# Seven-product expert blocks: sums behind the first layer on VectorE, first half's output sent a block later without drains, token rounding two blocks ahead

## The chip, the cores and the metric

One core of one Trainium2 chip runs one program. The metric is the device time of that program in microseconds; the time before is the median of three runs.

## The reference

```python
q_pool = q.reshape(B, H, S // 2, 2, D).mean(axis=3)          # B, H, S, D = 8, 8, 1152, 64
attn = softmax(q_pool @ k.T / sqrt(D))
x = (attn @ v) as (4608, 512) tokens
logits = x @ w_gate + modality_bias[modality_id]             # 8 experts
e_idx, gate_w = argmax(logits), its softmax probability
out[mask] = gate_w * (relu(x[mask] @ w1[e]) @ w2[e])         # per expert, w1 512x1024, w2 1024x512
```

All inputs and the output are float32.

## The kernel before, in words

The first two thirds of the time are the attention, in which TensorE is busy throughout; the change touches nothing there. Behind it stand the experts (function `experts`, L1375 on). The tokens are routed to experts and sorted into blocks of 256 tokens of one expert. `run_blocks` handles 18 such blocks and one with 32 leftover tokens. Every number is carried as a float16 high half and a float16 low half, so a product of two matrices takes three passes of TensorE (high x high, high x low, low x high).

Blocks 0 to 3 are plain blocks: four groups of first-layer products (`gemm1`) and four of the second layer (`gemm2`), which are the steps s = 0 to 7 of the loop. Blocks 4 to 17 replace the eight half-size products of each layer by seven, with sums of matrix quarters before and behind them (Winograd's form). Blocks 4 to 12 use one set of prepared weights (`sets[0]`), blocks 13 to 17 another (`sets[1]`). A set is prepared by `combined` (L1430): four quarters of a weight are loaded by SyncE into the pool `wr` of five raw buffers, GpSimd makes sums of them (L1433), and each of seven matrices is split: the high half by ScalarE (L1426), the low half by VectorE (L1427).

A block's tokens are prepared by `turn_s` (L1526), a generator of four steps: gates copied and the tokens scaled (ScalarE, `xr`, L1533); four subtractions on GpSimd (L1536); the cast to the high half (ScalarE, `xs`, L1540); the low half (VectorE, L1542) and two transposing DMAs of SyncE into `xpart` (L1545), a tile with two buffers. `load_x` gathers the tokens of a block with two indirect DMAs of GpSimd.

The loop over j from 4 to 17 works on two blocks at once. `together(j, j+1)` issues the first three first-layer products of block j+1 and then the seven second-layer products of block j (`second`); it yields six times, the steps s = 0 to 5. `tail(j+1)` issues the other four first-layer products and yields four times. So TensorE's order is: products 11, s2, s3 of block j+1 into banks `pa`, `pb`, `pc`; second-layer products 11, 22, 12, s3, s1, s2, s4 of block j; products 12, s1, 22, s4 of block j+1. Behind a first-layer product stand `first_sum` (VectorE, L1623), a relu (ScalarE, L1624), and, at the end of `tail`, four sums of the results (L1648, on GpSimd): `hs3`, `h21` (used as s1), `h11` (as s2) and `h12` (as s4). `put_hi` casts a result's high half (ScalarE, L1614), `put_lo` makes its low half (VectorE, L1618); `sums` does both for one of the four.

In `second`, ScalarE takes two scaled copies `p11`, `p12` of the first bank (L1718, `p` in the trace) before the third product adds into it, and another, `x5`, before the seventh product adds into that bank; VectorE adds up the output (L1719), and one quarter is added by GpSimd (L1741). `scatter` (L1592) writes half a block of output rows to the output with an indirect DMA of GpSimd; each scatter waits until the one before it has landed. In the loop the second half of block j is sent at step 4 of `together`, the first half in step 0 of `tail`, followed by `nc.gpsimd.drain`.

The order on TensorE, VectorE, ScalarE and GpSimd is the order of the program (`manual_schedule`); SyncE's DMAs are placed by the scheduler. PREP says how many steps of weight preparation run at each step s: its first part for the plain blocks, its second one tuple for each j from 4 on. T_TURN gives the steps at which block j+3's tokens advance, T_GX the step of the gather for block j+4.

Of the kernel before, what the change touches and what calls it, by code (L numbers as in the profile page):

```python
# [22 lines left out]
P = 128  # L23
# [88 lines left out]
GP = 10  # L112
WR = 5
JOINED = 2
PREP = ((1,) * 8, ((0, 1, 1, 0, 0, 0),) * 6 + ((0,) * 6, (1,) * 6, (1,) * 6) + ((1, 1, 1, 0, 0, 1),) * 4)
T_TURN = (0, 3, 5)
T_GX = 3
SIDE = 1
PH = 3
PO = 2  # L120
GX = 3
T_AHEAD = (6, 7)
T_OWN = ((1, 2), (2, 3))
T_ST = 5
LX = 0
SW = 3
PR = 2
# [42 lines left out]
def drain(g):  # L170
    for _ in g:
        pass
# [1202 lines left out]
def experts(tc, ctx, rt, ident, pre, x2pool, hip, w1, w2, out, side, first):  # L1375
# [54 lines left out]
    def combined(k, w, o, rooms):  # L1430

        rooms = iter(rooms)
        add = lambda o, a, b, op: nc.gpsimd.tensor_tensor(o, a, b, op=op)  # L1433
        put = lambda n, t: o.__setitem__(n, split(t, next(rooms)))
        if w is w1:
            c, a = load(k, w, 2), load(k, w, 3)
            yield
            t = wr.tile([P, 4 * TB], F32, name="raw", tag="w")
            add(t, c, a, ALU.add)
            b = load(k, w, 0)  # L1440
            yield
            put("22", a)
            d = load(k, w, 1)
            yield
            put("s1", t)
            yield
            add(c, b, c, ALU.subtract)
            yield
            put("s3", c)
            yield  # L1450
            add(t, t, b, ALU.subtract)
            yield
            put("11", b)
            yield
            put("s2", t)
            yield
            put("12", d)
            yield
            add(d, d, t, ALU.subtract)
            yield  # L1460
            put("s4", d)
            yield
        else:
            b, a = load(k, w, 1), load(k, w, 0)
            yield
            t = wr.tile([P, 4 * TB], F32, name="raw", tag="w")
            add(t, b, a, ALU.subtract)
            c = load(k, w, 3)
            yield
            put("11", a)  # L1470
            d = load(k, w, 2)
            yield
            put("t1", t)
            yield
            add(b, b, c, ALU.subtract)
            yield
            put("t3", b)
            yield
            add(t, c, t, ALU.subtract)
            yield  # L1480
            put("22", c)
            yield
            put("t2", t)
            yield
            put("21", d)
            yield
            add(d, d, t, ALU.subtract)
            yield
            put("t4", d)
            yield  # L1490
# [94 lines left out]

    def scaled(j, h):
        b = B[j]
        o = b["o", h] = xp.tile([P, DM], F32, name=f"o{h}", bufs=1)
        nc.scalar.activation(o, b["po"][h], AF.Copy, scale=b["gate"][:, h:h + 1])

    def scatter(j, h, n=P):
# [34 lines left out]
    def tail(j):  # L1626

        b = B[j]
        b["H"] = {}
        pa, pb, pc, u2, u3 = (b[n] for n in ("pa", "pb", "pc", "u2", "u3"))  # L1630
        product1(pa, "12", "21", j, False)
        h11 = b["h11"] = temp("h11")
        nc.scalar.activation(h11, pa, AF.Relu)
        yield
        product1(pb, "s1", "t1", j, True)
        first_sum(j, "h22", pb, u3)
        put_hi(j, "11", h11)
        yield
        product1(pc, "22", "t4", j, True)
        first_sum(j, "h12", pc, u3)  # L1640
        put_lo(j, "11", h11)
        put_hi(j, "22", b["h22"])
        yield
        product1(pb, "s4", "22", j, False)
        first_sum(j, "h21", pb, u2)
        h22, h12, h21 = (b[n] for n in ("h22", "h12", "h21"))
        b["hs3"] = temp("hs3")
        sub = lambda o, x, y, op=ALU.subtract: nc.gpsimd.tensor_tensor(o, x, y, op=op)  # L1648
        sub(b["hs3"], h21, h11)
# [8 lines left out]
    def sums(j, n):  # L1658
        t = B[j][dict(s3="hs3", s1="h21", s2="h11", s4="h12")[n]]
        put_hi(j, n, t)  # L1660
        put_lo(j, n, t)

    def together(i, j, scaling=iter(())):

        def mine(n):
            if i is not None:
                sums(i, n)

        if j is not None:
            b = B[j]  # L1670
            pa = b["pa"] = bank()
            product1(pa, "11", "11", j, True)
            p1 = temp("p1")
            nc.scalar.copy(p1, pa)  # L1674
            beside()
            step(scaling)
            mine("s3")
            pb = b["pb"] = bank()
            product1(pb, "s2", "t2", j, True)
# [4 lines left out]
            mine("s1")  # L1684
        else:
            mine("s3")
            mine("s1")
# [21 lines left out]
    def second(j):  # L1709
# [1 line left out]
        b = B[j]  # L1711
        g1, g2 = b["gate"][:, 0:1], b["gate"][:, 1:2]
        half = lambda n: temp(n, TB)
        o1, o2 = (xp.tile([P, DM], F32, name=f"o{h}", bufs=1) for h in range(2))
# [55 lines left out]
    def few_second(j):  # L1770
# [24 lines left out]
        for i in range(2):  # L1795
# [4 lines left out]
        o = b["o", 0] = xp.tile([P, DM], F32, name="o0", bufs=1)  # L1800
# [29 lines left out]
    def run_blocks():  # L1830
# [5 lines left out]
        raws = [load(0, w2, q) for q in range(4)]  # L1836
        load_x(1)
        turn = {1: turn_x(1)}
        prep = chain(combined(1, w1, sets[0]["w1"], (4, 5, 6, 7, 8, 13, 14)), combined(1, w2, sets[0]["w2"], (15, 16, 17, 18, 19, 20, 0)))
        for j in plain:  # L1840
            k = j + 2
            for s in range(8):
# [8 lines left out]
                beside()  # L1851
                if j == 0 and s in (1, 2):
                    step(turn[1])
                if j:
                    step(prep, PREP[0][s])
                if j and s == T_ST:
                    scatter(j - 1, 1)
                    nc.gpsimd.drain(fusable=False)
                if k <= NSA and s == GX:
                    load_x(k)  # L1860
                    turn[k] = (turn_x if k < NSA else turn_s)(k)
                if s in T_AHEAD and k <= NSA:
                    step(turn[k])
                if j == NSA - 1:
                    if s < 3:
# [4 lines left out]
                    if s > 3:  # L1870
                        step(turn[NSA + 1])
                    if s == 6:
                        load_x(NSA + 2)
            if j + 1 < NSA:
                drain(turn[j + 1])
# [12 lines left out]
                turn[k] = turn_s(k)  # L1888
        drain(together(None, j))
        step(turn[j + 2])  # L1890
        load_x(j + 3)
        step(turn[j + 2])
        scatter(j - 1, 1)
        for s, _ in enumerate(tail(j)):
            beside()
            if s == 1:
                step(turn[j + 2])
        drain(turn[j + 2])
        nc.gpsimd.drain(fusable=False)
        prep = chain(combined(0, w1, sets[1]["w1"], (1, 2, 3, 9, 10, 11, 12)), combined(0, w2, sets[1]["w2"], (7, 8, 6, 13, 5, 4, 14)), few_weights())  # L1900
        few_x_ = few_x()
        few1, few2 = few_first(NST), few_second(NST)
        for j in range(NSA, NST):
            if j == last:
                drain(few1)
            x = turn.get(j + 3, iter(()))
            for s, _ in enumerate(together(j, j + 1 if j < last else None, x)):
                beside()
                if s in T_TURN:
                    step(x)  # L1910
                if s == T_GX and j + 4 <= last:
                    if j + 4 == NA:
                        drain(side)
                    load_x(j + 4)
                if j == last - 1:
                    step(few_x_)
                step(prep, PREP[1][j - NSA][s] if j < last else 0)
                if s == 4:
                    scatter(j, 1)
            if j < last:  # L1920
                for s, _ in enumerate(tail(j + 1)):
                    beside()
                    beside()
                    if s == 0:
                        scatter(j, 0)
                        nc.gpsimd.drain(fusable=False)
        scatter(last, 0)
        nc.gpsimd.drain(fusable=False)
        drain(few2)
# [141 lines left out]
```

## Time and profile before

| | us |
|---|---|
| median of three runs | 1171.76 (1169.91 to 1172.52) |
| the profiled execution's own time | 1172.89 |
| its span, first to last instruction | 1171.2 |
| TensorE busy in the span | 1071.8 |
| GpSimd busy in the span | 639.9 |
| mean granted clock of TensorE | 0.97 |

The span is split into engines' busy times; a wait stands before the instruction that waited, with the instruction or DMA that released it. Releasers are inferred, and "issue" means that the profile shows none. The granted clock is the share of TensorE's full speed of 2.4 GHz.

### The profile page before, as it was taken

How to read it: one execution, taken by the hardware profiler on the slowest of the kernel's cores; microseconds unless marked ns; L12 is line 12 of the kernel's file. 1: busy time of each engine (PE TensorE's matmuls, PEld its weight loads, DVE VectorE, ACT ScalarE, POOL GpSimd, SP SyncE). 2: the span in 40 equal slices, each digit the busy share in tenths (PEclk: the TensorE clock that was granted, in tenths of full speed). 3: DMA queues.
4: the chain of work that ended last, by engine and by line, in shares of the span. 5: the costliest groups of instructions: out<-in, count | busy, mean ns of one | idle time of the engine just before them, and what ended most of it. 6: DMA issues, size and time to landing. Idle time of an engine off the chain costs nothing. (4 is left out here: it accounts for less than half of the span.)

```text
span 1171.2 us, 39664 instructions
## 1 busy us (share of the span) xinstructions
PE 1071.8 (92%) x16809; PEld 857.0 (73%) x16809; DVE 967.6 (83%) x1778; ACT 872.9 (75%) x1506; POOL 639.9 (55%) x610
## 2 busy tenths in 40 slices
PE   7999999999999999999999999997687789668985
PEld 3777777777777777777777779887676679567884
DVE  7999999999999999999999976895576666676773
ACT  5899999999999999999999985445545445545542
POOL 7855535445454554454554322477676666767443
PEclk9999999999999999999999999999989889889998
DMA  7688987886988787888788455445544335435210
GB/s 229 177 198 202 200 170 202 194 212 176 203 187 189 195 195 176 209 187 173 195 184 180 125 143 163 139 148 122 120 87 87 72 92 115 129 107 125 69 56 22
DMA packets 181868, 180.19 MB, mean 154 GB/s; under 512 B 113999, under 2 KB 144735, under 8 KB 181680
## 3 DMA queue, kind: packets, MB, share of 16 engines
q1 hardware_dynamic: 171414, 149.22, 52.7%
q0 software_dynamic: 10256, 28.33, 10.7%
q8 instruction: 133, 2.18, 0.8%
q14 instruction: 55, 0.45, 0.1%
q10 hardware_dynamic: 10, 0.00, 0.0%
HBM read 100.30 MB, written 18.98 MB: 102 GB/s over the span
## 5 line engine op out<-in xcount | busy, mean ns | idle before, releaser
L1024 ACT ACTIVATE Pe<-psc 128x432 int32<-128x432 f32 x768 | 376.4, 527 | 41.1 <-PE psc L1023 26.1
L1082 PE MATMUL xp<-VH,Pe 128*128 128x65 f16 x2880 | 345.3, 194 | 1.0 <-issue 1.0
L1083 PE MATMUL xp<-vl,Pe 128*128 128x64 f16 x2880 | 343.9, 192 | 0.5 <-issue 0.5
L1084 PE MATMUL xp<-VS,Pl 128*128 128x65 f16 x2880 | 343.3, 193 | 0.9 <-issue 0.5
L1082 PEld LDWEIGHTS <-Pe 128*128 128x128 f16 x2880 | 266.5, 97 | 94.2 <-issue 51.2
L947 DVE TENSOR_REDUCE mp<-pm 128x2 f32<-128x1024 f32 (+3 forms) x319 | 296.9, 938 | 19.7 <-PE pm L965 15.8
L1022 PE MATMUL psc<-B 128*128 128x432 f16 (+2 forms) x1152 | 302.2, 286 | 1.3 <-ACT Pe L1024 1.2
L1023 PE MATMUL psc<-B 128*128 128x432 f16 (+2 forms) x1152 | 299.6, 285 | 2.3 <-DMA B<-mr 2.3
L1083 PEld LDWEIGHTS <-Pe 128*128 128x128 f16 x2880 | 265.9, 98 | 44.1 <-issue 1.5
L1084 PEld LDWEIGHTS <-Pl 128*128 128x128 f16 x2880 | 266.2, 97 | 0.5 <-DVE Pl L1007 0.5
L1005 ACT ACTIVATE Pl<-Pe 128x1152 f16<-128x1152 uint16 x186 | 216.5, 1164 | 5.9
L868 POOL TENSOR_SCALAR VH<-rawv,sc 128x512 f16<-128x512 f32 (+1 forms) x60 | 104.0, 1733 | 42.4 <-DVE Pl L1007 37.9
L1023 PEld LDWEIGHTS <-B 128*128 128x128 f16 x1152 | 112.5, 98 | 10.5 <-issue 2.7
L1022 PEld LDWEIGHTS <-B 128*128 128x128 f16 x1152 | 111.2, 97 | 7.8 <-issue 2.4
L729 POOL TENSOR_TENSOR rawq<-rawq 128x576 f32<-128x576 f32 x31 | 43.7, 1409 | 118.8 <-DVE Pl L1007 113.3
L776 POOL TENSOR_TENSOR lo<-rawk,hi 128x576 f16<-128x576 f32 (+1 forms) x68 | 81.7, 1221 | 42.4 <-DVE Pl L1007 33.7
L1007 DVE TENSOR_SCALAR Pl<-Pe 128x576 f16<-128x576 uint16 (+1 forms) x198 | 93.1, 472 | 7.2 <-ACT Pe L1024 4.9
L947 DVE TENSOR_REDUCE mp<-xp 128x1 f32<-128x512 f32 x116 | 79.0, 681 | 0.0
L965 PE MATMUL pm<-hi,qh 64*128 64x512 f16 x348 | 70.0, 383 | 1.1 <-DVE mp L947 1.1
L1648 POOL TENSOR_TENSOR h<-h,h 128x512 f32<-128x512 f32 x42 | 64.0, 1524 | 3.3
L1536 POOL TENSOR_TENSOR xr<-xr 128x256 f32<-128x256 f32 x56 | 58.1, 1056 | 6.6 <-DVE w20l L1427 2.6
L1618 DVE TENSOR_TENSOR hs3l<-hs,hs3h 128x512 f16<-128x512 f32 x14 | 16.0, 1144 | 50.8 <-ACT hs3h L1614 50.8
(533 smaller groups left out, 2582.4 us busy)
## 6 DMA issues: line engine op xcount, KB each, us to landing
B<-hi SPq DMA_DIRECT2D x128, 144.0 KB
rawv<-in_att_dram SPq DMA_DIRECT2D x32, 576.0 KB
rawq<-in_att_dram SPq DMA_DIRECT2D x31, 576.0 KB
rawk<-in_att_dram SPq DMA_DIRECT2D x31, 576.0 KB
raw<-in_w_dram SPq DMA_DIRECT2D x28, 512.0 KB
B<-qh SPq DMA_DIRECT2D x128, 72.0 KB
B<-lo SPq DMA_DIRECT2D x64, 144.0 KB
xs<-x SPq DMA_DIRECT2D x15, 576.0 KB
```

The source lines that it names most:

```text
L776: done = (nc.gpsimd if p < 2 or i in LO_POOL else nc.vector).tensor_tensor(o[:, r], t[:, r], h[:, r], op=ALU.subtract)
L868: done = nc.gpsimd.tensor_scalar(vh, v, s["sc"], None, op0=ALU.mult)
L947: most = lambda o, x: nc.vector.tensor_reduce(o, x, op=ALU.max, axis=AX.X)
L965: nc.tensor.matmul(banks[to], queries(j, what), hi[half[j], t * 512:(t + 1) * 512], start=True, stop=True)
L1005: nc.scalar.activation(low, rest, AF.Copy, scale=LOW)
L1007: fast[0] = (nc.vector if eng == 'D' else nc.gpsimd).tensor_single_scalar(low, rest, LOW, op=ALU.mult)
L1022: nc.tensor.matmul(o, b1[:, ks], b1[:, qs], start=True, stop=False, skip_group_check=True)
L1023: nc.tensor.matmul(o, b2[:, ks], b2[:, qs], start=False, stop=True, skip_group_check=True)
L1024: nc.scalar.activation(Pe[:, D + x0:D + x1], pt, AF.Exp, scale=1.0 / 16)
L1082: nc.tensor.matmul(out, Ph[:, qs], vh[:, c, j, 0:D + 1], start=c == 0 and g == 0, stop=False, skip_group_check=True)
L1083: nc.tensor.matmul(out[:, 0:D], Ph[:, qs], vl[:, c, j], start=False, stop=False, skip_group_check=True)
L1084: nc.tensor.matmul(out, Pl[:, qs], vs[:, c, j, 0:D + 1], start=False, stop=c == NKC - 1, skip_group_check=True)
```

## The change

The four sums in `tail` go from GpSimd to VectorE, the fourth into `together`; `put_hi` and `put_lo` are interleaved by hand in `together` in place of `sums`. The first half of block j's output is sent at step 0 of block j+1, from a tile `o0` of two buffers; the drains in the loops are gone, and one is added before the last first half. In block j the tokens of block j+2 take their last two steps at step 0, those of block j+3 their first two at step 3, and the gather for block j+4 moves to step 4. Weight preparation starts in plain block 0, has steps in `tail`, is spread anew over the blocks, and makes two of its GpSimd sums in one step; the rooms that it writes to are numbered anew.

```diff
-PREP = ((1,) * 8, ((0, 1, 1, 0, 0, 0),) * 6 + ((0,) * 6, (1,) * 6, (1,) * 6) + ((1, 1, 1, 0, 0, 1),) * 4)
-T_TURN = (0, 3, 5)
-T_GX = 3
+PREP = (((0, 0, 0, 1, 1, 0, 1, 1), (1, 0, 1, 1, 1, 2, 0, 1), (1, 1, 0, 1, 1, 1, 0, 1), (1, 1, 2, 0, 1, 0, 0, 0)),
+        ((1, 0, 0, 0, 0, 1) + (0,) * 4, (0, 1, 1) + (0,) * 7, (0, 0, 0, 0, 0, 1) + (0,) * 4, (0, 1, 1) + (0,) * 7, (0, 1, 1, 0, 0, 1) + (0,) * 4,
+         (0, 1, 0, 0, 0, 2) + (0,) * 4, (0, 0, 0, 0, 0, 0) + (0,) * 4, (0, 1, 2, 0, 0, 1) + (0,) * 4, (0, 1, 1, 2, 0, 0, 0, 0, 0, 1)) + ((1, 1, 1, 0, 0, 1) + (0,) * 4,) * 4)
+T_NEAR = (0, 0)
+T_FAR = (3, 3)
+T_ST = 2
...
-T_ST = 5
...
     def combined(k, w, o, rooms):
...
+        if one:
+            add(c, b, c)
+            add(t, t, b)
         else:
...
+            add(c, c, b)
+            add(t, b, t)
+        yield
+        put(t3, c)
...
-        o = b["o", h] = xp.tile([P, DM], F32, name=f"o{h}", bufs=1)
+        o = b["o", h] = xp.tile([P, DM], F32, name=f"o{h}", bufs=2 - h)
...
-        sub = lambda o, x, y, op=ALU.subtract: nc.gpsimd.tensor_tensor(o, x, y, op=op)
+        sub = lambda o, x, y, op=ALU.subtract: nc.vector.tensor_tensor(o, x, y, op=op)
+        put_lo(j, "22", h22)
+        put_hi(j, "12", h12)
         sub(b["hs3"], h21, h11)
         sub(h21, h21, h22, ALU.add)
-        put_lo(j, "22", h22)
-        put_hi(j, "12", h12)
         put_lo(j, "12", h12)
         sub(h11, h21, h11)
-        sub(h12, h12, h11)
-        yield
...
     def together(i, j):
...
             nc.scalar.copy(p1, pa)
             beside()
-            step(scaling)
-            mine("s3")
+        hi("s3")
+        lo("s3")
+        hi("s1")
+        if i is not None:
+            nc.vector.tensor_tensor(B[i]["h12"], B[i]["h12"], B[i]["h11"], op=ALU.subtract)
+        lo("s1")
+        hi("s2")
+        if j is not None:
             pb = b["pb"] = bank()
...
         next(g, None)
-        mine("s2")
+        lo("s2")
+        hi("s4")
+        lo("s4")
         next(g, None)
-        mine("s4")
...
-                if j:
-                    step(prep, PREP[0][s])
+                step(prep, PREP[0][j][s])
                 if j and s == T_ST:
                     scatter(j - 1, 1)
-                    nc.gpsimd.drain(fusable=False)
...
-                    if s == 6:
+                    if s == 5:
                         load_x(NSA + 2)
...
-            x = turn.get(j + 3, iter(()))
-            for s, _ in enumerate(together(j, j + 1 if j < last else None, x)):
+            near, far = (turn.get(j + n, iter(())) for n in (2, 3))
+            for s, _ in enumerate(together(j, j + 1 if j < last else None)):
                 beside()
-                if s in T_TURN:
-                    step(x)
...
+                if s == 0 and j > NSA:
+                    scatter(j - 1, 0)
+                if s in T_NEAR and j + 2 <= last:
+                    step(near, T_NEAR.count(s))
+                step(prep, PREP[1][j - NSA][s] if j < last else 0)
+                if s in T_FAR:
+                    step(far, T_FAR.count(s))
+                if s == 4:
+                    scatter(j, 1)
+                    if j + 4 <= last:
...
             if j < last:
                 for s, _ in enumerate(tail(j + 1)):
                     beside()
                     beside()
-                    if s == 0:
-                        scatter(j, 0)
-                        nc.gpsimd.drain(fusable=False)
+                    step(prep, PREP[1][j - NSA][6 + s])
+        nc.gpsimd.drain(fusable=False)
         scatter(last, 0)
         nc.gpsimd.drain(fusable=False)
```

## Rows read from the trace of the kernel before

**Rows 1.** The page: busy time of each engine over the whole span
```profile
PE 1071.8 (92%) x16809; PEld 857.0 (73%) x16809; DVE 967.6 (83%) x1778; ACT 872.9 (75%) x1506; POOL 639.9 (55%) x610
```

**Rows 2.** Stretches: us; PE, PEld, DVE, ACT, POOL busy (count); granted clock; DMA share; GB/s
```profile
750.50:773.90 23.40, 21.76 (x213) 19.29 (x211) 22.98 (x48) 9.51 (x14) 9.49 (x6) 1.00 0.36 114
...
795.30:817.30 22.00, 15.37 (x242) 15.00 (x241) 8.95 (x12) 11.68 (x16) 17.01 (x17) 0.92 0.67 133
...
817.30:1145.60 328.30, 264.28 (x3305) 240.95 (x3303) 222.07 (x283) 163.24 (x266) 217.43 (x165) 0.92 0.40 95
...
973.10:991.80 18.70, 18.64 (x255) 17.57 (x253) 14.76 (x20) 11.05 (x19) 13.64 (x12) 1.00 0.39 92
...
1056.40:1076.50 20.10, 18.69 (x256) 17.62 (x253) 15.87 (x22) 12.56 (x20) 13.96 (x11) 1.00 0.46 125
...
1102.20:1121.40 19.20, 18.76 (x257) 17.64 (x254) 14.73 (x19) 10.45 (x18) 9.03 (x8) 1.00 0.20 52
...
1121.40:1145.60 24.20, 18.98 (x280) 17.02 (x278) 17.20 (x24) 10.92 (x21) 11.19 (x10) 0.93 0.16 46
```

**Rows 3.** Waits, 817.3 to 1145.6 us: total, times, longest
```profile
PE po L1707 <- ACT p L1718: 33.1, 10, 6.9
...
ACT hs3h L1614 <- POOL hs L1648: 32.8, 10, 7.0
...
POOL hs L1648 <- issue: 25.5, 7, 4.9
...
PE ph L1606 <- DVE h L1623: 16.1, 7, 8.4
```

**Rows 4.** Timeline of one block's start on POOL, ACT and PE
```profile
989.41 1.01 POOL L1592 DMA_INDIRECT out_dram<-o,siB  x1 [2.69 <-DVE h L1623]
...
993.92 1.26 POOL L1648 TENSOR_TENSOR hs<-h,h 128x512 f32<-128x512 f32 x1 [3.51 <-issue]
...
995.22 0.62 ACT L1614 CAST hs3h<-hs 128x512 f16<-128x512 f32 x1 [3.40 <-POOL hs L1648]
...
997.08 0.83 ACT L1718 ACTIVATE p<-po,gate 128x256 f32<-128x256 f32 x2
...
997.97 0.27 PE L1707 MATMUL po<-w20h,h12h 128*128 128x256 f16 x1 [3.34 <-ACT p L1718]
```

**Rows 5.** Drains behind the scatters of the first halves, ns min/median/max
```profile
L1926 POOLq DRAIN  x13: 3177/4447/6024, 837.9 to 1139.2; - x13
```

**Rows 6.** VectorE groups, 817.3 to 1145.6 us
```profile
L1542 DVE TENSOR_TENSOR xs<-xr,xs 128x1792 f16<-128x1792 f32 x12 | 30.2, 2516 | 0.0
...
L1618 DVE TENSOR_TENSOR hs1l<-h,hs1h 128x512 f16<-128x512 f32 x13 | 19.1, 1471 | 1.6
...
L1618 DVE TENSOR_TENSOR hs4l<-h,hs4h 128x512 f16<-128x512 f32 x13 | 12.6, 966 | 1.6
...
L1618 DVE TENSOR_TENSOR h22l<-h,h22h 128x512 f16<-128x512 f32 x13 | 8.9, 682 | 0.0
...
L1427 DVE SCALAR_TENSOR_TENSOR w9l<-raw,w9h 128x1024 f16<-128x1024 f32 x2 | 2.4, 1216 | 0.0
```

**Rows 7.** GpSimd groups, 817.3 to 1145.6 us
```profile
L1648 POOL TENSOR_TENSOR h<-h,h 128x512 f32<-128x512 f32 x40 | 61.2, 1529 | 3.1
...
L1536 POOL TENSOR_TENSOR xr<-xr 128x256 f32<-128x256 f32 x44 | 48.4, 1119 | 1.6 <-ACT p L1718 0.7
```

**Rows 8.** TensorE timeline of the first seven-product block: its two longest waits
```profile
803.04 0.27 PE L1606 MATMUL ph<-xpart,w13h 128*128 128x128 f16 x2 [3.54 <-ACT p L1674]
...
811.86 0.37 PE L1606 MATMUL ph<-xpart,xt 128*128 128x128 f16 x2 [2.42 <-DMA xpart<-xs]
```

**Rows 9.** SyncE: a transposing DMA, and its waits ahead of weight loads
```profile
804.58 1.88 SPq L1545 DMA_TRANSPOSE xpart<-xs  x1
...
L1421 SPq EVENT_SEMAPHORE  x6: 17/17/8572, 1004.1 to 1064.2; - x6
```

**Rows 10.** The chain of waits at the kernel's end
```profile
1157.59 2.74 DMA out_dram<-o,siB
```

More of the change, by code (lines that the diff above doesn't have):

```diff
@@ L1432, in combined @@
         rooms = iter(rooms)
-        add = lambda o, a, b, op: nc.gpsimd.tensor_tensor(o, a, b, op=op)
+        add = lambda o, a, b, op=ALU.subtract: nc.gpsimd.tensor_tensor(o, a, b, op=op)
         put = lambda n, t: o.__setitem__(n, split(t, next(rooms)))
-        if w is w1:
-            c, a = load(k, w, 2), load(k, w, 3)
-            yield
[L1438 to L1462, printed above, removed]
-        else:
[L1464 to L1490, printed above, removed]
@@ new lines, in combined @@
+        one = w is w1
+        first_, t1, t2, t3, t4 = ("22", "s1", "s2", "s3", "s4") if one else ("11", "t1", "t2", "t3", "t4")
+        mid, last_ = ("11", "12") if one else ("22", "21")
+        c, a = load(k, w, 2 if one else 1), load(k, w, 3 if one else 0)
+        yield
+        t = wr.tile([P, 4 * TB], F32, name="raw", tag="w")
+        add(t, c, a, ALU.add if one else ALU.subtract)
+        b = load(k, w, 0 if one else 3)
+        yield
+        put(first_, a)
+        d = load(k, w, 1 if one else 2)
@@ L1492, in load_x @@
+        yield
+        put(t1, t)
+        yield
+        if one:
+            add(c, b, c)
+            add(t, t, b)
+        else:
+            add(c, c, b)
+            add(t, b, t)
+        yield
+        put(t3, c)
+        yield
+        put(mid, b)
+        yield
+        put(t2, t)
+        yield
+        put(last_, d)
+        yield
+        add(d, d, t)
+        yield
+        put(t4, d)
+        yield
     def load_x(j):
@@ L1647, in tail, with together @@
         b["hs3"] = temp("hs3")
-        sub = lambda o, x, y, op=ALU.subtract: nc.gpsimd.tensor_tensor(o, x, y, op=op)
+        sub = lambda o, x, y, op=ALU.subtract: nc.vector.tensor_tensor(o, x, y, op=op)
+        put_lo(j, "22", h22)
+        put_hi(j, "12", h12)
         sub(b["hs3"], h21, h11)
         sub(h21, h21, h22, ALU.add)
-        put_lo(j, "22", h22)
-        put_hi(j, "12", h12)
         put_lo(j, "12", h12)
         sub(h11, h21, h11)
-        sub(h12, h12, h11)
         yield
[L1658 to L1667, printed above, removed]
+    def together(i, j):
+        hi, lo = ((lambda n, f=f: i is not None and f(i, n, B[i][dict(s3="hs3", s1="h21", s2="h11", s4="h12")[n]])) for f in (put_hi, put_lo))
         if j is not None:
@@ L1713, in second @@
         half = lambda n: temp(n, TB)
-        o1, o2 = (xp.tile([P, DM], F32, name=f"o{h}", bufs=1) for h in range(2))
+        o1, o2 = (xp.tile([P, DM], F32, name=f"o{h}", bufs=2 - h) for h in range(2))
         b["o", 0], b["o", 1] = o1, o2
@@ L1799, in few_second @@
             turned.append(px)
-        o = b["o", 0] = xp.tile([P, DM], F32, name="o0", bufs=1)
+        o = b["o", 0] = xp.tile([P, DM], F32, name="o0", bufs=2)
         g = b["gate"][ts, 0:1]
@@ L1838, in run_blocks @@
         turn = {1: turn_x(1)}
-        prep = chain(combined(1, w1, sets[0]["w1"], (4, 5, 6, 7, 8, 13, 14)), combined(1, w2, sets[0]["w2"], (15, 16, 17, 18, 19, 20, 0)))
+        prep = chain(combined(1, w1, sets[0]["w1"], (13, 14, 4, 5, 6, 7, 8)), combined(1, w2, sets[0]["w2"], (15, 16, 17, 18, 19, 20, 0)))
         for j in plain:
@@ L1853, in run_blocks @@
                     step(turn[1])
-                if j:
-                    step(prep, PREP[0][s])
+                step(prep, PREP[0][j][s])
                 if j and s == T_ST:
                     scatter(j - 1, 1)
-                    nc.gpsimd.drain(fusable=False)
                 if k <= NSA and s == GX:
                     load_x(k)
-                    turn[k] = (turn_x if k < NSA else turn_s)(k)
+                    turn[k] = turn_x(k) if k < NSA else turn_s(k)
                 if s in T_AHEAD and k <= NSA:
@@ L1864, in run_blocks @@
                 if j == NSA - 1:
-                    if s < 3:
+                    if s < 2:
                         step(turn[NSA])
@@ L1869, in run_blocks @@
                         turn[NSA + 1] = turn_s(NSA + 1)
-                    if s > 3:
-                        step(turn[NSA + 1])
-                    if s == 6:
+                    if s > 2:
+                        step(turn[NSA + 1], (1, 1, 0, 1, 1)[s - 3])
+                    if s == 5:
                         load_x(NSA + 2)
@@ L1890, in run_blocks @@
         step(turn[j + 2])
+        step(turn[j + 2])
         load_x(j + 3)
-        step(turn[j + 2])
         scatter(j - 1, 1)
-        for s, _ in enumerate(tail(j)):
+        for _ in tail(j):
             beside()
-            if s == 1:
-                step(turn[j + 2])
-        drain(turn[j + 2])
-        nc.gpsimd.drain(fusable=False)
-        prep = chain(combined(0, w1, sets[1]["w1"], (1, 2, 3, 9, 10, 11, 12)), combined(0, w2, sets[1]["w2"], (7, 8, 6, 13, 5, 4, 14)), few_weights())
+        prep = chain(combined(0, w1, sets[1]["w1"], (1, 2, 3, 9, 10, 11, 12)), combined(0, w2, sets[1]["w2"], (5, 6, 4, 14, 13, 7, 8)), few_weights())
         few_x_ = few_x()
@@ L1905, in run_blocks @@
                 drain(few1)
-            x = turn.get(j + 3, iter(()))
-            for s, _ in enumerate(together(j, j + 1 if j < last else None, x)):
+            near, far = (turn.get(j + n, iter(())) for n in (2, 3))
+            for s, _ in enumerate(together(j, j + 1 if j < last else None)):
                 beside()
-                if s in T_TURN:
-                    step(x)
[L1911 to L1914, printed above, removed]
+                if s == 0 and j > NSA:
[8 more added lines that the diff above has]
+                    if j + 4 <= last:
+                        if j + 4 == NA:
+                            drain(side)
+                        load_x(j + 4)
                 if j == last - 1:
                     step(few_x_)
-                step(prep, PREP[1][j - NSA][s] if j < last else 0)
-                if s == 4:
-                    scatter(j, 1)
             if j < last:
@@ L1923, in run_blocks @@
                     beside()
-                    if s == 0:
-                        scatter(j, 0)
-                        nc.gpsimd.drain(fusable=False)
+                    step(prep, PREP[1][j - NSA][6 + s])
+        nc.gpsimd.drain(fusable=False)
         scatter(last, 0)
```

4 lines of the change are left out of this document (removed).

## The prediction

> **What bounds the kernel now.** I read the page first [rows 1]: TensorE is busy 92% of the span, so only a stretch where it is not can give much. The busy time by stretch [rows 2] finds it. The attention and the four plain blocks run at full clock with hardly a gap; the 13 periods from the first second-layer product of block 4 to that of block 17 last 328.3 us, of which TensorE works 264.3. A period without a wait exists: 973.1 to 991.8 takes 18.7 us, 18.64 of them busy, at granted clock 1.00. So 13 x 18.64 = 242 us is what the products cost; 64 us are idle, and about 22 us more are products that ran slowly: the granted clock of the stretch is 0.92, so some 16% of it was at 1.2 instead of 2.4 GHz, and the three quiet periods, without long waits, have 1.00. A wait here is paid about one and a third times.
>
> The waits say who is late [rows 3]. TensorE waits longest for ScalarE's `p` (33.1 us, 10 times): the two scaled copies of the first second-layer bank, which the third product adds into. ScalarE isn't slow; its queue has `hs3h` in front, which waits 32.8 us, 10 times, for GpSimd's first sum. And 25.5 us of GpSimd's idle time ahead of that sum has no releaser. One block shows the chain [rows 4]: the scatter of a first half starts at 989.41 and takes 1.01, then GpSimd stands 3.51 us although the operands are there, sums from 993.92, ScalarE casts at 995.22 and scales at 997.08, and TensorE resumes at 997.97 after 3.34 us. What holds GpSimd is the drain behind the scatter, 3.2 to 6.0 us in each of 13 blocks [rows 5]. The sums themselves are four in a row of 1.3 to 1.5 us [rows 4, 7].
>
> **The change, part by part.** Profiled execution: 1172.89 us, 1.1 above the median of the three runs; the sum is made against the former.
>
> 1. *Sums to VectorE.* Four per block, 52 in the stretch, leave GpSimd. The trace has no VectorE sum of three f32 tiles in SBUF. From below the price is that of `h22l`, same size and undisturbed: 0.68 us [rows 6]; from above GpSimd's own 1.53 [rows 7]. I take 0.69, nearest in engine and size. On the other side the four low halves, made while GpSimd sums, take 1.47 to 0.97 us (the groups from `hs1l` to `hs4l`, 65.2 us together) against 0.68 for the same operation undisturbed [rows 6]. With the sums gone they should return to 0.69: 65.2 - 35.9 = 29.3 us saved against 35.9 spent. VectorE's busy time goes from 222.1 [rows 2] to 228.7 us. 22 of its weight splits at 1.22 [rows 6] are 26.8 of this, so a block costs 15.5 us plus 1.22 per split: 17.9 with two, 19.2 with three, 20.4 with four. TensorE's 18.64 is longer except in the eighth and ninth of these blocks, which hold three and four.
>
> 2. *Late casts.* A sum no longer waits for a drain or for GpSimd's queue. Counted from the end of the last first-layer product, at 0.69 a VectorE step [rows 6] and 0.62 a cast [rows 4]: first_sum, relu, a low half and the first two sums end by 3.3, `hs3h` and `hs1h` by 4. A product is 18.64/14 = 1.33 us; the fourth ends at 5.3, `p` takes 0.83 [rows 4] and is done at 6.2, and TensorE wants it at 6.6. The 33.1 us go. What is late next is VectorE's in-order queue: h22's first_sum must be done within one product of 1.33 us, and the splits stand in front of it.
>
> 3. *Scatters and drains.* The drains in the loop go (13 behind first halves, and those of the plain blocks). The first half is sent at step 0 of the next block, from a second buffer, when it has long been finished; the second half still at step 4. Each scatter waits for the one before to land, 2.7 us [rows 10], now half a block earlier, so nothing. On GpSimd, behind the scatter at step 0 stand weight sums and the four `xr` subtractions, needed a block later: no cost. Behind the one at step 4 stand two gathers, also needed a block later.
>
> 4. *Token rounding two blocks ahead.* Steps 3 and 4 of block j+2 (ScalarE cast, VectorE subtraction of 2.5 us [rows 6], two transposing DMAs) run at step 0, steps 1 and 2 of block j+3 at step 3. The transposes no longer wait on SyncE for TensorE to leave the operand buffer, and the weight loads behind them go earlier. The price is slack: thirteen VectorE steps of 0.69 stand in front of the subtraction, so it ends 11 to 11.5 us into the block, and the DMA issued at 804.58 landed when TensorE resumed at 811.86, 7.3 us [rows 8, 9]: at 18.3 to 18.8 the tokens are there, just when TensorE wants them. At best a landing costs nothing, at worst a block pays 2 to 3 us. I take zero, since that DMA stood in the busiest stretch, with a DMA share of 0.67 against 0.40 later [rows 2]. In the last four blocks SyncE has a weight load behind the transposes whose split follows one step later on ScalarE, ahead of the copy `x5` that the seventh product needs: if the load really goes last, up to 5 us in each of four blocks, which I keep for the range.
>
> 5. *Preparing weights.* 22 steps start one block sooner, in block 0. In the stretch 750.5 to 773.9 VectorE is busy 22.98 of 23.4 us [rows 2]; two splits fewer there lets TensorE's 21.4 set it: -2 us (bounds 0 and -2.2).
>
> 6. *First seven-product block.* 22.0 us for ten products, 10 x 1.33 = 13.3 us. It waits 3.54 us for a copy queued behind the last weight split, and 2.42 for tokens of the next block [rows 8]; the split now comes before the block, and the tokens are rounded one step earlier. Bounds 0 and -8.6; I take -7.
>
> 7. *End.* A drain is added before the last first half, which has to wait for the landing in front anyway [rows 10]; the leftover tokens' output has its own buffer. Within 1 us either way: 0.
>
> **Sum.** The quiet periods take 18.7, 20.1 and 19.2 us [rows 2], mean 19.3. Twelve such are 231.6; the ninth block's four splits add 1; the thirteenth holds the leftover tokens' first layer, 24.2 us with 18.98 busy [rows 2], and I leave it 23. Together 255.6, that is 72.7 less. 1172.9 - 72.7 - 7 - 2 = 1091.2; less the 1.1 to the median: **1090 us**. From below, thirteen periods of 18.64 and the bounds of 5 and 6 give 1075.
>
> **Rivals.**
>
> *VectorE becomes the bound* (0.20). GpSimd keeps `xr`, 48.4 us in the stretch at 1.12 each [rows 7], and the new sums read two SBUF tiles as the slow low halves did. If low halves stay at 65.2 and the sums cost 0.69, a block averages (222.1 + 35.9)/13 = 19.8; if they cost 1.53, 23.2. In the middle, 21.5: 279 us for the stretch, so about 1114; at the upper end 302, about 1136. Against it: `h22l` is not slowed where GpSimd rests, and `xr`'s 48.4 is less than the 61.2 of `h` alone that goes [rows 7]. The Trainium skill (SBUF — State Buffer, section SBUF: two separate sides) says that a VectorE operation with two SBUF inputs and a GpSimd operation take turns on a shared pair, the loser standing for the whole instruction; by it all 48.4 us of `xr` could be added to 228.7, 277 us and about 1112. The trace agrees in kind: 1.47 against 0.68 us [rows 6].
>
> *Tokens late* (0.11). If VectorE slips by 2 us and landings take 7.3, TensorE waits some 2.5 us at each block's start and loses 2 more at 1.2 GHz: 13 x 23.2 = 302 us, about 1137.
>
> *The drains were not the cause* (0.04): `p` stays late behind VectorE's sums. The 33.1 us [rows 3] stay and 17 of the slow clock with them; 1090 + 50 = 1140.
>
> *Slower* (0.03). SyncE's queue holds weight loads, one of which waited 8.57 us for its buffer [rows 9]. If such a load stands ahead of the transposes in every block, tokens land 8.6 us late: 18.7 + 8.6 + 2.5 of slow clock = 29.8, 387 us, about 1222. It decides from a period of 25.9 us on, a wait of about 5 us per block. Against it: the buffers' users are finished a block earlier now.
>
> **Chances.** 0.60 for the forecast, the rest as above, 0.02 for no effect that can be measured. Range 1075 to 1132: both bounds of the forecast and most of the first rival. Less than 0.2% (2.3 us) can't be told from no change here. Faster 0.95, same 0.02, slower 0.03.
>
> **What would show it.** Right: TensorE's wait for `p` below 5 us in the stretch, no drain between blocks, hs1l at 0.7, clock 0.98 or more, periods of 18.7 to 20. VectorE above 95% busy with TensorE waiting for first_sum is the first rival; TensorE waiting for DMA at the first product of a block is the second. The forecast is wrong if the 13 periods last over 275 us.

## The result, and the profile after

| | us |
|---|---|
| before, median of four runs | 1170.84 (1166.78 to 1172.52) |
| after, median of four runs | 1095.33 (1094.57 to 1096.08) |
| after / before | 0.936 (0.9334 to 0.9386) |
| the profiled execution after: own time, span | 1096.08, 1094.3 |
| 13 periods from block 4 to block 17, before, after | 328.3, 256.3 |

The forecast was 1090. The two spans differ by 76.9 us: the 13 periods give 72.0, the first seven-product block 7.7, and the plain blocks start 2.4 earlier; plain block 2 takes back 4.6 and the end 0.5. The 2.4 can't be put down to an edit: no edit touches the attention in front of the blocks, and in the runs below, none of which touches it either, block 0 starts anywhere from 703.1 to 709.5 us.

The page of the kernel after, busy time of each engine, to be set beside [rows 1]:

```profile
PE 1052.4 (96%) x16809; PEld 844.7 (77%) x16809; DVE 980.1 (90%) x1834; ACT 871.1 (80%) x1506; POOL 538.0 (49%) x554
```

Four stretches after, columns as in [rows 2]: plain block 2, the first seven-product block, the 13 periods, and the longest of them:

```profile
748.20:776.10 27.90, 23.36 (x212) 20.11 (x210) 27.70 (x47) 8.89 (x13) 15.97 (x10) 0.94 0.42 110
797.50:811.80 14.30, 13.56 (x242) 13.42 (x241) 10.07 (x16) 9.69 (x17) 9.13 (x9) 1.00 0.75 177
811.80:1068.10 256.30, 243.92 (x3303) 228.78 (x3301) 226.51 (x333) 161.54 (x264) 118.06 (x112) 0.99 0.48 123
868.80:893.60 24.80, 21.45 (x255) 18.99 (x252) 21.20 (x30) 14.35 (x23) 11.32 (x11) 0.86 0.41 106
```

GpSimd's busy time in the periods has fallen from 217.4 [rows 2] to 118.1, TensorE's from 264.3 to 243.9 for the same products, at a granted clock of 0.99 against 0.92. Waits in the 13 periods after, columns as in [rows 3]:

```profile
PE po L1680 <- ACT p L1691: 8.1, 5, 3.3
...
PE ph L1585 <- DVE h L1602: 1.5, 2, 1.3
```

The 33.1 us that TensorE waited for `p` [rows 3] are 8.1, in 5 blocks. VectorE's groups in the periods, to be set beside [rows 6]: the new sums (L1627, L1650), the tokens' subtraction (L1521) and one of the low halves:

```profile
L1627 DVE TENSOR_TENSOR h<-h,h 128x512 f32<-128x512 f32 x26 | 25.0, 963 | 0.4
L1521 DVE TENSOR_TENSOR xs<-xr,xs 128x1792 f16<-128x1792 f32 x12 | 24.2, 2016 | 0.0
L1627 DVE TENSOR_TENSOR hs<-h,h 128x512 f32<-128x512 f32 x13 | 16.0, 1229 | 1.3
...
L1650 DVE TENSOR_TENSOR h<-h,h 128x512 f32<-128x512 f32 x13 | 8.9, 682 | 0.0
...
L1597 DVE TENSOR_TENSOR hs1l<-h,hs1h 128x512 f16<-128x512 f32 x13 | 8.8, 681 | 0.0
```

`hs1l` is back from 1.47 to 0.68 us. The sum that is issued in `together` costs 0.68 as well; the three issued in `tail` have means of 0.96 and 1.23. Their excess is in few instructions. The timeline of the block with the longest period, on the four engines:

```profile
866.28 4.67 POOL L1435 TENSOR_TENSOR raw<-raw 128x1024 f32<-128x1024 f32 x2
866.32 5.19 DVE L1627 TENSOR_TENSOR hs<-h,h 128x512 f32<-128x512 f32 x1
...
871.54 0.62 ACT L1593 CAST hs3h<-hs 128x512 f16<-128x512 f32 x1 [4.26 <-DVE hs L1627]
...
874.88 0.37 PE L1680 MATMUL po<-w20h,h12h 128*128 128x256 f16 x1 [3.35 <-ACT p L1691]
```

VectorE's sum starts 0.04 us behind two weight sums of GpSimd and is done only when both are. ScalarE's cast waits 4.26 for it, the copies `p` stand behind the cast, and TensorE waits 3.35; the period, which has a mean granted clock of 0.86, takes 24.8 us. The chain is that of [rows 4], with GpSimd's weight sums in the drain's place. In the 13 periods seven VectorE instructions stand in this way, together 14.6 us beyond their undisturbed length (0.69 for a sum, 1.22 for a split); five of them stand beside a weight sum `raw`, in the five blocks in which TensorE waits for `p`. The Trainium skill (SBUF — State Buffer, section SBUF: two separate sides) says that a VectorE operation with two SBUF inputs and a GpSimd operation that reads SBUF exclude each other for a whole instruction. The trace agrees; here the loser stood for two instructions in a row, 5.19 us.

Plain block 2 shows the same. Timeline after, VectorE and TensorE, then GpSimd:

```profile
750.71 1.74 DVE L508 TENSOR_TENSOR more<-more,ok 128x36 f32<-128x36 f32 x1
...
754.70 3.11 DVE L519 TENSOR_SCALAR hii<-ri 128x36 int32<-128x36 int32 x1
...
759.71 0.68 DVE L1547 SCALAR_TENSOR_TENSOR h11l<-ph,h11h 128x512 f16<-128x512 f32 x1
...
760.45 0.27 PE L1541 MATMUL ph<-xpart,w2h 128*128 128x256 f16 x1 [4.27 <-DVE h11l L1547]
...
749.86 2.55 POOL L1435 TENSOR_TENSOR raw<-raw 128x1024 f32<-128x1024 f32 x1 [7.11 <-issue]
754.35 1.02 POOL L1571 DMA_INDIRECT out_dram<-o,siA  x1 [1.95 <-ACT o L1568]
755.40 2.35 POOL L1435 TENSOR_TENSOR raw<-raw 128x1024 f32<-128x1024 f32 x1
```

Two small steps of the routing list, 0.2 us each elsewhere in the trace, take 1.74 and 3.11 until a weight sum ends (752.41 and 757.75); the second starts while GpSimd issues a scatter and stands through that and the sum behind it. `h11l` is queued behind both steps, TensorE waits 4.27 for it, and the block's mean granted clock falls to 0.94. Before, with the preparation a block later, one weight sum lay ahead of `h11l`, ending 0.4 us before block 2 begins, the next came 17 us after it, and TensorE waited 1.14 (GpSimd's timeline of the kernel before, then TensorE's):

```profile
747.62 2.49 POOL L1433 TENSOR_TENSOR raw<-raw 128x1024 f32<-128x1024 f32 x1 [4.99 <-DVE x L1427]
...
764.62 2.51 POOL L1433 TENSOR_TENSOR raw<-raw 128x1024 f32<-128x1024 f32 x1 [12.53 <-issue]
...
759.68 0.27 PE L1562 MATMUL ph<-xpart,w2h 128*128 128x256 f16 x1 [1.14 <-DVE h11l L1568]
```

### The profile page after: what moved, and what is told of

It is laid out like the page before. It is cut to its first block, busy times and chain, and to the rows that moved or that the text cites. A ratio compares the mean times of both kernels' runs of the same rounds, so it can differ in the third digit from the quotient of the medians.

```text
span 1094.3 us, 39595 instructions
## 1 busy us (share of the span) xinstructions
PE 1052.4 (96%) x16809; PEld 844.7 (77%) x16809; DVE 980.1 (90%) x1834; ACT 871.1 (80%) x1506; POOL 538.0 (49%) x554
## 5 line engine op out<-in xcount | busy, mean ns | idle before, releaser
L1515 POOL TENSOR_TENSOR xr<-xr 128x256 f32<-128x256 f32 x56 | 45.6, 833 | 80.1 <-ACT xr L1512 63.8
L1435 POOL TENSOR_TENSOR raw<-raw 128x1024 f32<-128x1024 f32 x16 | 38.4, 2407 | 35.3 <-DVE gate L1478 15.8
L740 POOL CAST qh<-rawq 128x576 f16<-128x576 f32 x30 | 19.9, 664 | 64.7 <-DVE Pl L1009 41.4
```

## The experiments

"13" is the sum of the 13 periods, "block 2" the plain block's period, in the profiled execution. Ratios are to the kernel before, on the same chip. The runs come from three chips, on which the kernel before has medians from 1169.4 to 1176.5 us, and the attention alone moves the start of block 0 by microseconds; so where a few us matter, the 13 periods are compared.

| run | median | ratio, 95% | 13 | block 2 |
|---|---|---|---|---|
| before_no_drains | 1148.86 | 0.9791 (0.9731 to 0.9851) | 301.0 | 23.4 |
| before_vector_sums | 1126.42 | 0.9602 (0.9545 to 0.9659) | 281.9 | 23.4 |
| after_gpsimd_sums | 1142.15 | 0.9741 (0.9682 to 0.98) | 302.0 | 28.0 |
| after_with_drains | 1108.98 | 0.9447 (0.939 to 0.9504) | 268.6 | 28.0 |
| after_tokens_three_ahead | 1108.94 | 0.9477 (0.9436 to 0.9518) | 271.0 | 28.0 |
| after_weight_sums_apart | 1083.48 | 0.9264 (0.9232 to 0.9296) | 244.3 | 27.9 |
| after_plain_spread | 1094.51 | 0.9358 (0.9327 to 0.939) | 254.1 | 27.6 |
| after_both | 1083.04 | 0.9261 (0.9229 to 0.9292) | 243.8 | 27.6 |
| apart_plain_late | 1078.43 | 0.9229 (0.9202 to 0.9256) | 244.4 | 22.1 |
| apart_plain_late_even | 1079.67 | 0.923 (0.9203 to 0.9257) | 244.3 | 22.1 |
| late_with_drains | 1090.65 | 0.9288 (0.9229 to 0.9347) | 254.6 | 22.1 |
| late_tokens_three | 1109.05 | 0.945 (0.9387 to 0.9512) | 269.9 | 21.8 |

**One part alone, on the kernel before.** Without the drain of the loop:

```diff
                         scatter(j, 0)
-                        nc.gpsimd.drain(fusable=False)
```

> The kernel before without the 13 drains behind the first halves, all else as it was; the scatter still waits for the one before to land and the sums still run on GpSimd. Theory F: the 25.5 us without a releaser and some slow clock go: 1135 to 1150 us. Rival D: 1115 or less. Rival S: 1160 or more.

With the sums of `tail` on VectorE and all else as before:

```diff
-        sub = lambda o, x, y, op=ALU.subtract: nc.gpsimd.tensor_tensor(o, x, y, op=op)
+        sub = lambda o, x, y, op=ALU.subtract: nc.vector.tensor_tensor(o, x, y, op=op)
```

> The kernel before with its four sums on VectorE, drains and all else as they were. Theory F: the casts no longer stand behind a drain, most of the 33.1 us for p goes with half of the slow clock, while late tokens' subtractions, weight steps and VectorE's order stay: 1115 to 1135 us. Rival D: 1155 or more. Rival S: 1105 or less.

Both met theory F's figures: 27.3 and 46.4 us off the 13 periods. TensorE's waits there, first of the one, then of the other:

```profile
PE ph L1606 <- DVE h L1623: 18.0, 8, 8.4
...
PE po L1707 <- ACT p L1718: 10.6, 5, 6.9
```

```profile
PE ph L1606 <- DVE h L1623: 20.2, 8, 6.5
PE po L1707 <- ACT p L1718: 4.2, 1, 4.2
```

Either edit takes most of the 33.1 us [rows 3], so they overlap: the drain delayed the sums, and sums on another engine no longer stand behind it. What both leave is VectorE's late first sum `h`, 16.1 us before [rows 3], 18 and 20 here, 1.5 in the kernel after. In the kernel before, all seven of these waits come behind the tokens' subtraction `xs` in VectorE's queue, some with a weight split in between. Its longest, on VectorE, then on TensorE:

```profile
1011.65 3.64 DVE L1542 TENSOR_TENSOR xs<-xr,xs 128x1792 f16<-128x1792 f32 x1
...
1016.36 1.27 DVE L1623 TENSOR_TENSOR h<-ph,u 128x512 f32<-128x512 f32 x2
...
1017.09 0.37 PE L1606 MATMUL ph<-xpart,w14h 128*128 128x128 f16 x2 [8.39 <-DVE h L1623]
```

**One part undone, on the kernel after.** All four sums back on GpSimd (`sub` in `tail` as above, the other way round, and in `together`):

```diff
-            nc.vector.tensor_tensor(B[i]["h12"], B[i]["h12"], B[i]["h11"], op=ALU.subtract)
+            nc.gpsimd.tensor_tensor(B[i]["h12"], B[i]["h12"], B[i]["h11"], op=ALU.subtract)
```

> The changed kernel with its four sums per block back on GpSimd, at the same places, without drains. Theory F (the forecast's: drains and the sums' engine both hold the casts): the low halves slow down again to 1.0 to 1.5 us and the chain to hs2h and hs4h is 3 us longer, so some waits for p return: 1110 to 1125 us. Rival D (only drains and the scatter's place mattered): 1090 to 1102. Rival S (only the engine of the sums mattered): 1130 or more.

1142, as rival S had it, and 17 us above theory F's figures: the engine of the sums is worth 47 us even without a drain in front. The old chain is back whole, without its drain:

```profile
PE po L1680 <- ACT p L1691: 33.0, 13, 5.4
...
ACT hs3h L1593 <- POOL hs L1627: 17.2, 13, 4.3
```

The 13 periods take 302.0, against 301.0 in before_no_drains, which has the same sums on GpSimd and no drain in the loop either: with the sums there, the other parts of the change together give nothing. TensorE's wait for `h` falls from 18.0 to 0.7, and that for `p` rises from 10.6 to 33.0.

The drain back behind the scatter at step 0:

```diff
                 if s == 0 and j > NSA:
                     scatter(j - 1, 0)
+                    nc.gpsimd.drain(fusable=False)
```

> The changed kernel with a drain behind the scatter at step 0 of every block. Theory F: GpSimd stands some 3 us, but nobody waits for it there: 1093 to 1100 us. Rival D (a drain in the loop costs whatever stands behind it): 1110 or more.

1109, 13.7 more (12.3 in the 13 periods), a microsecond short of rival D's figure and 9 above theory F's. Not by the old chain: the wait for `p` is 9.0 against 8.1. New are waits of TensorE inside first-layer products for nothing that the profile shows:

```profile
PE po L1680 <- ACT p L1691: 9.0, 5, 2.7
PE ph L1585 <- issue: 5.8, 17, 1.0
```

The rounding back to one pass, three blocks ahead:

```diff
-T_NEAR = (0, 0)
-T_FAR = (3, 3)
+T_TURN = (0, 0, 3, 5)
...
-            near, far = (turn.get(j + n, iter(())) for n in (2, 3))
+            x = turn.get(j + 3, iter(()))
...
-                if s in T_NEAR and j + 2 <= last:
-                    step(near, T_NEAR.count(s))
+                if s in T_TURN:
+                    step(x, T_TURN.count(s))
...
-                if s in T_FAR:
-                    step(far, T_FAR.count(s))
...
```

> The changed kernel with the tokens rounded three blocks ahead again (two steps at step 0, the cast at step 3, the subtraction and the transposes at step 5; transposes wait on SyncE until TensorE leaves the operand buffer). Theory F (this part was priced at zero): 1092 to 1102 us, SyncE waits of 10 us and more return but no one needs the tokens. Rival T (rounding two ahead frees the queues and is worth more): 1108 or more, TensorE or ScalarE waiting for weight splits.

1109, which is rival T's figure, and the 13 periods 14.7 us longer. What is late is neither a transfer nor, as T had it, a weight split, but VectorE's queue. TensorE's wait in the periods, then the timeline of the worst case on GpSimd, VectorE and TensorE:

```profile
PE ph L1584 <- DVE h L1601: 17.8, 12, 4.4
```

```profile
963.21 5.67 POOL L1434 TENSOR_TENSOR raw<-raw 128x1024 f32<-128x1024 f32 x2
...
966.72 4.03 DVE L1520 TENSOR_TENSOR xs<-xr,xs 128x1792 f16<-128x1792 f32 x1
970.68 1.74 DVE L1428 SCALAR_TENSOR_TENSOR x<-raw,x 128x1024 f16<-128x1024 f32 x1
972.34 1.27 DVE L1601 TENSOR_TENSOR h<-ph,u 128x512 f32<-128x512 f32 x2
...
973.07 1.22 PE L1584 MATMUL ph<-xpart,xfirst 128*128 128x128 f16 x10 [4.42 <-DVE h L1601]
```

At step 5 the subtraction of the tokens (2.0 us, here 4.03 beside GpSimd) stands in front of `h`, in the part of the block where TensorE needs an `h` per product; at step 0 it does not. Eight of the 12 waits, 11.9 of the 17.8 us, come behind it. The other four come behind the low half `h11l`, which takes 3.3 to 5.6 us in place of 0.7 beside a weight sum.

**GpSimd's weight sums away from the block's head.** The second set is prepared by a copy of `combined` that makes one GpSimd sum per step, and every such sum is issued at step 3, behind the token subtractions:

```diff
-        ((1, 0, 0, 0, 0, 1) + (0,) * 4, (0, 1, 1) + (0,) * 7, (0, 0, 0, 0, 0, 1) + (0,) * 4, (0, 1, 1) + (0,) * 7, (0, 1, 1, 0, 0, 1) + (0,) * 4,
+        ((1, 0, 0, 1, 0, 0) + (0,) * 4, (0, 0, 0, 1, 0, 0) + (0,) * 4, (0, 1, 1, 1, 0, 0) + (0,) * 4, (0, 1, 1, 0, 0, 0) + (0,) * 4, (0, 1, 1, 1, 0, 0) + (0,) * 4,
...
-                step(prep, PREP[1][j - NSA][s] if j < last else 0)
                 if s in T_FAR:
                     step(far, T_FAR.count(s))
+                step(prep, PREP[1][j - NSA][s] if j < last else 0)
```

> The changed kernel with the eight GpSimd sums of the second weight set put one to a block at step 3, behind the xr subtractions, so that they no longer run while VectorE begins a block. Theory L (what is left of TensorE's waits for p comes from VectorE's sums standing while GpSimd sums weights: 5.19, 3.32 us instead of 0.69): the waits for p go, 1082 to 1089 us. Rival Q (VectorE's load or the p copies themselves are late): within 2 us of the changed kernel.

1083.5, 12 less than the kernel after, within theory L's figures. The 13 periods and VectorE's sums there:

```profile
810.70:1055.00 244.30, 240.33 (x3302) 227.17 (x3300) 214.73 (x334) 161.56 (x265) 124.26 (x112) 1.00 0.50 129
```

```profile
L1663 DVE TENSOR_TENSOR h<-h,h 128x512 f32<-128x512 f32 x26 | 17.9, 688 | 0.4
...
L1663 DVE TENSOR_TENSOR hs<-h,h 128x512 f32<-128x512 f32 x13 | 9.0, 692 | 1.3
```

The sums cost the forecast's 0.69, no wait for `p` is left, and TensorE is busy 240.3 of 244.3 us at a granted clock of 1.00.

**Plain block 2.** First with fewer splits in it:

```diff
-PREP = (((0, 0, 0, 1, 1, 0, 1, 1), (1, 0, 1, 1, 1, 2, 0, 1), (1, 1, 0, 1, 1, 1, 0, 1), (1, 1, 2, 0, 1, 0, 0, 0)),
+PREP = (((0, 0, 0, 1, 1, 0, 1, 1), (1, 1, 1, 1, 1, 2, 1, 1), (0, 1, 0, 1, 0, 1, 0, 1), (1, 1, 2, 0, 1, 0, 0, 0)),
```

> The changed kernel with weight preparation in the plain blocks moved from block 2 to block 1 (9 and 4 steps instead of 7 and 6). Theory V (block 2 takes 27.9 us because VectorE is busy 27.7 of them with splits, routing lists and stands behind GpSimd's weight sums): block 2 back to 22 to 24 us, 1088 to 1092 us. Rival R (the routing lists alone fill VectorE there): within 1 us of the changed kernel.

> Both of the moves before this together. Theories L and V: the gains add, 1076 to 1084 us.

Block 2 stayed at 27.6 in both, so theory V failed: the number of VectorE's splits is not the cause. after_plain_spread lies 0.8 us below the kernel after, as rival R had it; after_both, 1083.0, lies inside its figures without the second gain, 0.4 below after_weight_sums_apart. The timeline of after_plain_spread shows other steps of the list standing beside the weight sums that the edit moved there:

```profile
748.34 4.66 POOL L1435 TENSOR_TENSOR raw<-raw 128x1024 f32<-128x1024 f32 x2 [4.54 <-issue]
```

```profile
748.60 2.14 DVE L501 TENSOR_TENSOR row<-row,pos 128x36 f32<-128x36 f32 x1
750.66 2.66 DVE L493 SCALAR_TENSOR_TENSOR ohp<-ohp,done 128x288 f32<-128x288 f32 x1
```

So, on after_weight_sums_apart, the sums were put behind block 2's gathers, which wait for the list:

```diff
-PREP = (((0, 0, 0, 1, 1, 0, 1, 1), (1, 0, 1, 1, 1, 2, 0, 1), (1, 1, 0, 1, 1, 1, 0, 1), (1, 1, 2, 0, 1, 0, 0, 0)),
+PREP = (((0, 0, 0, 1, 1, 0, 1, 1), (1, 0, 1, 1, 1, 1, 0, 0), (0, 0, 0, 0, 1, 1, 1, 1), (2, 1, 1, 1, 1, 1, 1, 1)),
```

> The version with the second set's weight sums apart, with the first set's GpSimd sums moved too: in plain block 2 no weight sum stands ahead of the gathers of step 3 in GpSimd's queue (the list of steps per block becomes 4, 5, 4, 9 in place of 4, 7, 6, 5). Theory L (GpSimd's weight sums at the head of block 2 hold VectorE's routing list, and with it the low half h11l that TensorE waits 4.3 us for): the stands ahead of h11l go (1.7 for 0.2 and 3.1 for 0.2 us in the profile of the changed kernel, 4.5 together), block 2 falls from 27.9 to 23.4 to 25 us, the time to 1077 to 1081 us; up to 3 us may come back in block 3 and the fill, where the splits of the second weight now crowd. Rival R (the routing list alone is too long, the sums only lie beside it): block 2 stays at 27 to 28 us and the time at 1082 to 1086.

> The same with the steps of the first set spread 4, 5, 5, 8 and none in step 0 of block 3. Theory L: block 2 as in the run beside it (23.4 to 25 us), the time 1077 to 1081; the sums at the end of block 2 stand before VectorE's list of block 3 in both, so the two agree within 2 us. Rival R: block 2 at 27 to 28 us, 1082 to 1086.

Both times, 1078.4 and 1079.7, are theory L's, and rival R is out: the block takes 22.1 in both, below the 23.4 to 25 that L named and 5.8 less than in after_weight_sums_apart, with four and five steps of preparation in it where after_plain_spread had four and took 27.6. Of the 5.8, 2.7 and 2.4 come back in the fill, the first seven-product block (14.1 to 16.8 and 16.5). apart_plain_late is 16.9 us below the kernel after. In its block 2 VectorE still stands, but later, where nothing waits for it. The stretch, then GpSimd, then VectorE:

```profile
746.80:768.80 22.00, 21.65 (x212) 19.18 (x210) 21.79 (x44) 5.95 (x10) 13.27 (x10) 1.00 0.31 92
```

```profile
755.84 4.68 POOL L1435 TENSOR_TENSOR raw<-raw 128x1024 f32<-128x1024 f32 x2
```

```profile
752.74 0.68 DVE L1583 SCALAR_TENSOR_TENSOR h11l<-ph,h11h 128x512 f16<-128x512 f32 x1
...
755.16 5.78 DVE L538 TENSOR_TENSOR ol<-lof,lane 128x384 bf16<-128x384 bf16 x2
```

**The two undone parts again, without the weight sums in the way.** The same two edits on apart_plain_late:

> The version with all weight sums moved (apart_plain_late, 1078.4 us) with a drain behind the scatter of step 0 again, as in after_with_drains, which cost 13.7 us. There TensorE waited 5.8 us, 17 times, for nothing that the profile shows, in first-layer products, and no longer than before for VectorE or ScalarE. Theory Y (the drain costs by itself, whatever stands behind it on GpSimd): the same waits without a releaser come again, 13 periods of 251 to 258 us together and 1086 to 1094. Theory X (it cost by shifting GpSimd's weight sums against VectorE's work): with the sums behind the token subtractions it costs under 5 us, 1077 to 1083.

> The same version with the rounding of tokens three blocks ahead at steps 0, 0, 3, 5, as in after_tokens_three_ahead, which cost 13.6 us; there TensorE waited 17.8 us, 12 times, for VectorE's first-layer sum h. Theory Q (the 2.0 us subtraction of the low half at step 5 stands in VectorE's queue in front of the sums of the four products of the tail, which have 1.33 us each): the waits for h stay at 10 us or more, 1088 to 1096. Theory L (it cost by GpSimd's work holding that subtraction and others, 4.0 us for 2.0 in the eighth block): with the weight sums moved the waits fall under 5 us and the time is 1078 to 1084.

Theory Y holds (254.6 and 1090.7): the drain adds 10.2 us to the 13 periods here and 12.3 on the kernel after, so it does not act by shifting the weight sums. The three-ahead rounding adds 25.5 to them, against 14.7 on the kernel after: with it they take 269.9 and 271.0, whatever GpSimd's weight sums do. (The medians, 12.2 and 30.6 us above apart_plain_late, are from another chip.) TensorE's waits from 800 us on, of late_with_drains, then of late_tokens_three:

```profile
PE ph L1621 <- issue: 6.5, 17, 1.0
```

```profile
PE ph L1620 <- DVE h L1637: 11.7, 9, 3.6
PE ph L1620 <- issue: 7.1, 17, 1.1
```

The waits for `h` stay above 10 us, as theory Q said, all nine of them behind the tokens' subtraction, but the time is 13 us above its figures. Part of that are the same waits without a releaser as behind the drain, in a kernel with no drain between blocks; after_gpsimd_sums, which has no such drain either, has 12 of them, 3.2 us. So the drain is not what they need.

They go with the gathers: in after_with_drains, late_with_drains and late_tokens_three each of the 17 ends 0.6 to 3.3 us after the start of a gather. In the quiet stretches of the traces the matmuls of a first-layer product start 56 ns apart. Those that start 0.4 to 3.4 us after a gather does are later than that by 9.5 us in all in each of the two runs with drains (waits for a named engine not counted). That is most of the 12.3 and 10.2 that the drain costs. It is 12.8 in late_tokens_three, and nothing in the kernel after and in apart_plain_late. Why is open: these two issue the same gathers at the same step, and no run here moved the gathers alone.

## Why the prediction was right, point by point

The bottleneck was named rightly: drain, late sum, late cast, late `p`. The 13 periods took 256.3 us, forecast 255.6, and the signs it gave came: no wait for a transfer at a block's start, `hs1l` at 0.68, granted clock 0.99, periods of 18.5 to 19.8 in eleven of 13 (the others took 24.8, the timeline above, and 21.7, the eighth). One sign failed, the wait for `p`, and within the sum errors cancelled; that 256.3 lies so near 255.6 is in part luck. The fourth and eighth period took 7.9 us more than the forecast's mean of 19.3 each; against that the thirteenth took 19.5 for 23, the ninth 18.9 for 20.3, and the other nine 2.4 less together.

1. *Sums to VectorE.* 0.69 holds for a VectorE sum with GpSimd quiet (0.682 in `together`, 0.688 and 0.692 in after_weight_sums_apart) and not beside its weight sums: the 52 cost 49.9 us, not 35.9. The low halves fell as said. The tokens' subtraction fell from 30.2 [rows 6] to 24.2 and the low half `h12l` from 12.1 to 8.9, which were not in the sum, and records of VectorE that follow each other overlap by up to 0.1 us. So VectorE's total, 226.5, met the forecast's 228.7 although the sums cost 14 us more.
2. *Late casts.* "The 33.1 us go" was too much: 8.1 stayed, over the sign's 5. The first rival held the mechanism, VectorE standing beside GpSimd, but charged it to the token subtractions `xr`. Those lie where VectorE is seldom late: one split in the eighth block took 1.70 for 1.22 beside them. It is the weight sums, 2.37 us each and up to two in a row at the block's head, for which the forecast had no term; moved, they give 12 us.
3. *Scatters and drains.* The scatters cost nothing that can be seen: apart_plain_late sends them at the same steps, and TensorE is busy 240.4 of its 244.4 us. That the drains' removal acts only through the sums was wrong: with the sums on VectorE a drain costs 12.3 and 10.2 us in the periods, by a mechanism that stays open.
4. *Tokens.* The price of zero was right, and so was leaving the late weight loads out: the last four blocks take 19.1, 18.6, 18.5 and 19.5. That the step also gains was missing: undone, it costs 14.7 us in the periods, mostly by VectorE's queue. The 16.1 us of waits for `h` [rows 3], all behind the tokens' subtraction, are taken by no step of the forecast; they are left out only by its sum over quiet periods.
5. *Preparing weights: the failed term.* -2 forecast, +4.6 measured. The step counted VectorE's busy 22.98 of 23.4 us [rows 2] as work that could move away. Some of it was standing beside GpSimd (two steps of the list took 2.10 and 2.59 for 0.55 there), and the preparation that starts a block sooner put two of GpSimd's weight sums ahead of `h11l`, where one had been. after_plain_spread shows that the splits' number does not matter, apart_plain_late that the sums' place does.
6. *First seven-product block:* 14.3 us, -7.7 for -7.
7. *End:* 0.5 more, within the microsecond allowed.

The time lies 5.3 us above the forecast: term 5 is 6.6 of it (the 4.6, and the 2 that did not come), the periods 0.7 and the end 0.5; the fill (0.7) and the earlier start (2.4, which is luck) take some back, and the 0.6 left is rounding and the difference between the profiled executions and the medians.

## What to carry to other kernels

Work that is started earlier, or freed from a wait, lands somewhere else on every engine that it uses: ask beside which VectorE instructions. GpSimd arithmetic on large SBUF tiles belongs behind an instruction that waits for the last urgent VectorE step of the block; where it lies matters more than how much it is (the same eight sums in another step gave 12 us). When VectorE is "busy", compare the instruction's mean with its shortest before counting it as work.

## What the runs showed of the hardware that was not expected

A VectorE instruction can stand beside GpSimd for far more than its own length, and for more than one GpSimd instruction: 5.19 us for 0.69, behind two sums of 2.37; 3.11, through the issue of a scatter and a weight sum, for a 128x36 integer operation with one tile as its input that takes 0.18 in the kernel before. A drain on GpSimd that follows an issued scatter lasted 3.1 to 8.3 us in after_with_drains, as against 3.2 to 6.0 [rows 5], and cost 12.3 and 10.2 us in the periods although the waits that it adds to TensorE have no releaser in the profile. First-layer products lost 6 to 7 us in 17 short waits that no profile row explains, all of them within 3.3 us behind a gather, in three programs, and none in the kernel after and in apart_plain_late, which issue the same gathers at the same step.
